# Decays laid out chunk by chunk, paired exponentials and 1 MB loads in a gated recurrence with a convolution-gated projection

## The chip, the cores and the metric

One core of a Trainium2 chip. The metric is the device time of one execution in microseconds (us); it is measured as the median of several runs. The program has five compute streams that run their own instruction queues in order and meet only at semaphores: TensorE (PE in the profile, with its weight loads as PEld), VectorE (DVE), ScalarE (ACT), GpSimd (POOL) and the queue that issues the DMAs (SP).

## The reference

Two layers over x of shape 4 x 6336 x 256 (batch, time, features), all float32.

```python
# layer 1: gated linear recurrence
a_base = 1/(1+exp(-a_param)); sig_r = 1/(1+exp(-r_gate)); sig_i = 1/(1+exp(-i_gate))
a_t  = exp(8 * sig_r * log(clip(a_base, 1e-6, 1-1e-6)))
norm = sqrt(max(1 - a_t*a_t, 1e-6))
h    = a_t[:, t] * h + (norm * sig_i * x)[:, t]        # over t; y[:, t] = h
# layer 2: on y
gate = 1/(1+exp(-causal_conv_5(y, conv_w)))            # 5 taps, each feature by itself
out  = (gate * (y @ w_val)) @ w_out
```

## The kernel before, in words

The 4 x 6336 = 25344 time steps stand in one row. They are cut into 51 windows (`w`, 512 steps, some 256) and 28 chunks (`c`): chunks 0, 1, 2, 26 and 27 are one window each, chunks 3 to 25 are two windows, 1024 steps. The 256 features are two halves `h` of 128.

Inputs arrive with time on the partitions. For a chunk the program does this, each step an operation with a short name in a hand-written order:

- `lr`, `li`, `lx` (SP): load a window of r_gate, i_gate and x, 512 KB, each partition a run of 4 rows (4 KB), into rings of four windows (`rring`, `iring`, `xring`).
- `ta`, `tb` (ACT): tanh of half the gates, for a whole chunk, to `taring` and `tbring` in bf16. The sigmoids are made from these.
- `tr` (PE): transposes of `taring`, so that features stand on the partitions; `ex` (ACT): the decays a_t = exp(k tanh + k), out of PSUM into `aring`, one instruction for each half of a chunk, or of a pair of chunks where `GROUPS` puts two together.
- `sq` (POOL): a squared, into `ering`; two of them are `sa`, on ACT. `rt` (ACT): sqrt(0.25 - 0.25 a²) for a batch of chunks (`BATCHES`, mostly three). Sqrt lies in another function table than tanh and exp, so an `ACT_TABLE_LOAD` stands before each batch and another before the next tanh or exp.
- `pp` (POOL): tanh + 1; `up` (POOL): times x, into `uring`. For three early windows PE and DVE do it (`xp`, `uv`).
- `nt` (PE): transposes of the square roots back to time on the partitions; two bf16 values are moved as one 4-byte element. `xg` (DVE): `uring` times them. `xt` (PE): transposes of that, features on the partitions. For the last two chunks (`LAST`) it is done the other way round.
- `sc` (DVE): the recurrence, a scan over a chunk for each half, into `yring`.
- `cv` (PE): the five taps as small diagonal matmuls; `tg` (ACT): tanh of it; `vl` (PE): y @ w_val; `gv` (DVE): (tanh + 1) times that; `ou` (PE): times w_out; `cd` (DVE) or `ca` (ACT): copy out of PSUM into `oring`; `st` (SP): store of a window, 512 KB.
- `wm` (PE): five matmuls of the identity, whose result nobody reads. There are 17 of them.

The table `ORDER` lists all operations in one sequence. Each engine executes its own in that sequence, so the table sets what stands behind what in each queue; semaphores put in by the framework do the rest. A word is `name.chunk.half` or `name.window`, and `@` gives the PSUM banks.

The transposes of `nt` read `ering` with a step, because time step and partition are dealt out by `p j`:

```python
nc.tensor.transpose(out=bank[:, k:k + P], in_=ering[:, e + q:e + wins[w] // 2:nq], identity=ident[:])
```

With windows of 512 steps nq is 2, so the 4-byte elements that are read lie 8 bytes apart; with 256 it is 1.

Of the kernel before, what the change touches and what calls it, by code (L numbers as in the profile page):

```python
# [9 lines left out]
P = 128  # L10
# [4 lines left out]
ALU = mybir.AluOpType  # L15

CHUNKS = [[256], [256], [512], [512, 512], [512, 512], [512, 512], [512, 512], [512, 512], [512, 512], [512, 512],
    [512, 512], [512, 512], [512, 512], [512, 512], [512, 512], [512, 512], [512, 512], [512, 512], [512, 512],
    [512, 512], [512, 512], [512, 512], [512, 512], [512, 512], [512, 512], [512, 512], [512], [256]]
BATCHES = [[0], [1], [2], [3, 4], [5, 6, 7], [8, 9, 10], [11, 12, 13], [14, 15, 16], [17, 18, 19], [20, 21, 22],  # L20
    [23, 24, 25], [26, 27]]
NA = 5120
# [16 lines left out]
s_ident s_small s_kt s_diag lr.2 lr.0 s_wl.3 lr.1 li.0 lr.3 s_wl.2 ta.2 ta.0 lr.4 tr.0.1@0 tr.2.0@1 lr.6 ta.1 lr.5  # L39
tr.1.0@2 tb.0 tr.0.0@3 li.1 tr.2.1@4 ex.2.0 li.2 tr.1.1@5 li.3 ex.1.1 lx.0 ex.0.1 sq.1.1 li.4 ex.1.0 sq.2.0 ex.0.0  # L40
ex.2.1 sq.1.0 ta.3 sq.2.1 pp.0 sq.0.0 sq.0.1 ta.4 tb.1 lr.10 tr.3.0@4,5 tb.2 lr.9 lr.8 lr.7 lx.2 tr.3.1@2,3 ex.3.0
s_wl.1 up.0 lx.1 lx.4 wm.10@6 ex.3.1 sq.3.0 wm.5@6 lx.3 wm.3@6 tb.3 sq.3.1 wm.9@6 wm.6@6 ta.6 pp.4 sq.4.1 ta.5 lr.13
li.5 xp.2@2,3 li.6 sq.4.0 li.7 lr.14 tr.5.0@4,5 lx.6 uv.2 pp.3 rt.0 rt.2 nt.0@0 up.4 xg.0 rt.1 xt.0@0,1 xp.1@2 rt.3
sc.0.0 nt.1@3 up.3 lx.5 nt.2@0 uv.1 s_wl.0 xg.1 xg.2 xt.1@2,3 sc.0.1 lx.7 sc.1.0 nt.3@6,7 lr.12 sc.1.1 xg.3 ex.5.0
xt.2@0,1 sc.2.1 sc.2.0 tb.4 cv.0@2,3 tr.5.1@4,5 xt.3@6,7 lr.11 li.8 sq.5.0 ex.5.1 tg.0 sc.3.0 pp.5 sc.3.1 cv.2@0,1
s_wcast cv.1@4,5 ta.8 xp.6@2,3 uv.6 vl.0@6,7 tg.1 tg.2 vl.2@0,1 up.5 ta.7 sq.6.1 lx.8 li.9 li.10 lr.17 lr.18
nt.4@2,3 gv.0 tb.5 tr.7.0@6,7 ou.0.0@4 gv.2 ex.7.0 xg.4 sq.6.0 cd.0.0 tr.7.1@0,1 sq.5.1 vl.1@2,3 ou.2.0@4,5 ex.7.1
# [59 lines left out]
def kernel(  # L107
# [34 lines left out]
    def places(cap, lens):  # L142
# [6 lines left out]
        return out  # L149

    group_of = {c: g for g in GROUPS for c in g}
    a_at = places(NA, clen)
    e_at = places(NE, clen)

    segs, y_at, y_wrap = [], [], []
# [34 lines left out]
    with tc.manual_schedule():  # L190
# [103 lines left out]
        def op_lr(w):  # L294
            load(w, "r")
# [298 lines left out]
```

## Time and profile before

| | |
|---|---|
| median of 3 runs | 287.65 us (287.34, 287.65, 289.22) |
| span of the profiled execution | 286.4 us; its own time is not listed apart, so the median of the runs, 1.25 us more, stands for it |
| busy: PE, DVE, ACT, POOL | 251.8, 246.8, 273.6, 241.6 us |
| bytes moved | 104.76 MB, mean 366 GB/s; HBM read 78.39 MB, written 25.95 MB |
| granted TensorE clock, mean | 0.999 |

The busy time of an engine is the union of its instructions, from the profiler; an instruction can start before the one ahead of it has ended, so the durations of a group add up to more. Idle time before an instruction is put down to what ended it. The chain of waits follows the work back from the last instruction. Times in the views count from the first instruction of the span.

### The profile page before, as it was taken

What the parts mean: (1) busy time and instruction counts of PE and PEld (TensorE: products, weight loads), DVE (VectorE), ACT (ScalarE), POOL (GpSimd) and SP (SyncE); (2) the same over time, 40 slices, a digit from 0 to 9 for tenths busy, and PEclk for the clock granted to TensorE, in tenths of its full rate; (3) what the DMA queues carried; (4) which work ended last, traced back from release to release, by engine and by line L of the source; (5) the groups of instructions that cost most, each with busy time, mean ns of one, the idle gap of its engine ahead of it and who ended that gap; (6) DMA issues with size and microseconds to landing.
All of it is one profiled execution on the core that took longest, in us unless ns stands there. A gap on an engine that the chain in (4) does not pass through costs nothing.

```text
span 286.4 us, 6382 instructions
## 1 busy us (share of the span) xinstructions
PE 251.8 (88%) x2552; PEld 171.1 (60%) x2576; DVE 246.8 (86%) x214; ACT 273.6 (96%) x198; POOL 241.6 (84%) x161
## 2 busy tenths in 40 slices
PE   1387778899999999988988999989989899999993
PEld 1253447456656767455756676656646774767562
DVE  4002898969999899999999999999999999999991
ACT  5999999999999999999999999999999999898984
POOL 1659589899999999999999999999996999874600
PEclk9999999999999999999999999999999999999999
DMA  7999999999999999999999999999999999994536
GB/s 243 384 373 407 409 403 408 388 366 376 410 408 366 418 367 392 414 410 334 405 364 413 411 332 356 420 416 419 415 401 333 359 416 406 364 356 170 192 150 256
DMA packets 29996, 104.76 MB, mean 366 GB/s; under 512 B 3335, under 2 KB 3854, under 8 KB 29966
## 3 DMA queue, kind: packets, MB, share of 16 engines
q1 hardware_dynamic: 29952, 104.35, 94.5%
q8 instruction: 20, 0.33, 0.5%
q14 instruction: 10, 0.08, 0.1%
q10 hardware_dynamic: 14, 0.01, 0.0%
HBM read 78.39 MB, written 25.95 MB: 364 GB/s over the span
## 4 chain that ended last, share of the span: by engine, by line
ACT 33%; PE 29%; DVE 14%; issue 12%; DMA 8%; SPq 1%; ACTq 0%; DVEq 0%
ACT ering L405 8%; PE banks L495 8%; DVE yring L483 7%; PE banks L525 7%; DMA rring<-in_r_gate_dram 6%; ACT tgring L502 6%; ACT taring L310 5%; ACT tbring L313 5%; ACT aring L378 5%; PE banks L510 5%; PE banks L461 3%; DVE tgring L515 3%; PE banks L420 3%; ACT L562 3%; DVE oring L533 2%
## 5 line engine op out<-in xcount | busy, mean ns | idle before, releaser
L386 POOL TENSOR_TENSOR ering<-aring 128x1024 f32<-128x1024 f32 (+2 forms) x54 | 91.5, 1714 | 16.7 <-ACT aring L378 16.4
L332 POOL TENSOR_TENSOR uring<-tbring,xring 128x1024 bf16<-128x1024 bf16 (+1 forms) x48 | 101.1, 2119 | 3.6 <-DMA xring<-in_x_dram 3.1
L483 DVE TENSOR_TENSOR_SCAN yring<-aring,yring,banks 128x1024 bf16<-128x1024 f32 (+5 forms) x50 | 101.7, 2064 | 2.1 <-PE banks L461 1.9
L495 PE MATMUL banks<-yring,diag 64*64 64x512 bf16 (+7 forms) x1080 | 62.1, 361 | 2.3 <-ACT aring L378 1.6
L515 DVE SCALAR_TENSOR_TENSOR tgring<-tgring,banks 128x1024 bf16<-128x1024 bf16 (+1 forms) x51 | 59.1, 1178 | 4.0 <-PE banks L510 3.4
L320 POOL TENSOR_SCALAR tbring<-tbring 128x1024 bf16<-128x1024 bf16 (+1 forms) x48 | 49.1, 1032 | 6.8 <-ACT tbring L313 6.7
L378 ACT ACTIVATE aring<-banks,khf 128x2048 f32<-128x2048 bf16 (+3 forms) x38 | 54.2, 1476 | 0.4 <-PE banks L357 0.3
L525 PE MATMUL banks<-wo,tgring 128*128 128x256 bf16 x396 | 51.0, 274 | 3.7 <-DVE tgring L515 3.2
L502 ACT ACTIVATE tgring<-banks 128x1024 bf16<-128x1024 f32 (+1 forms) x51 | 50.2, 1011 | 2.0 <-PE banks L495 1.9
L510 PE MATMUL banks<-yring,wv 128*128 128x512 bf16 (+4 forms) x192 | 48.1, 359 | 3.7 <-ACT tgring L502 1.9
L310 ACT ACTIVATE taring<-rring 128x2048 bf16<-128x2048 f32 (+2 forms) x28 | 47.9, 1718 | 1.4 <-DMA rring<-in_r_gate_dram 1.4
L525 PEld LDWEIGHTS <-tgring 128*128 128x128 bf16 x396 | 41.2, 114 | 13.1 <-DVE tgring L515 8.8
L313 ACT ACTIVATE tbring<-iring 128x2048 bf16<-128x2048 f32 (+2 forms) x28 | 48.2, 1726 | 0.0
L405 ACT ACTIVATE ering<-ering 128x4096 bf16<-128x4096 f32 (+5 forms) x16 | 44.8, 2840 | 0.1
L495 PEld LDWEIGHTS <-diag 64*64 64x64 bf16 x1080 | 29.0, 106 | 25.6 <-issue 9.9
L533 DVE COPY oring<-banks 128x1024 f32<-128x1024 f32 (+1 forms) x36 | 41.9, 1182 | 1.4 <-PE banks L525 0.7
L357 PE MATMUL banks<-ident_b,taring 128*128 128x128 bf16 x396 | 29.9, 230 | 9.4 <-ACT taring L310 6.7
L357 PEld LDWEIGHTS <-taring 128*128 128x128 bf16 x396 | 26.5, 103 | 14.2 <-ACT taring L310 7.4
L510 PEld LDWEIGHTS <-wv 128*128 128x128 bf16 x216 | 19.7, 98 | 24.5 <-issue 10.3
L450 DVE TENSOR_TENSOR uring<-banks,uring 128x2048 bf16<-128x2048 bf16 (+2 forms) x26 | 29.4, 1134 | 3.5 <-PE banks L420 3.2
L420 PE MATMUL banks<-ident,ering 128*128 128x128 f32 x192 | 28.3, 289 | 1.1 <-ACT ering L405 0.9
L461 PE MATMUL banks<-ident,uring 128*128 128x128 f32 x192 | 25.9, 276 | 3.5 <-DVE uring L450 2.8
(49 smaller groups left out, 154.0 us busy)
## 6 DMA issues: line engine op xcount, KB each, us to landing
rring<-in_r_gate_dram SPq DMA_DIRECT2D x48, 512.0 KB, 8.2
iring<-in_i_gate_dram SPq DMA_DIRECT2D x48, 512.0 KB, 8.7
xring<-in_x_dram SPq DMA_DIRECT2D x48, 512.0 KB, 8.2
out_dram<-oring SPq DMA_DIRECT2D x48, 512.0 KB, 6.5
rring<-in_r_gate_dram SPq DMA_DIRECT2D x3, 256.0 KB, 4.1
iring<-in_i_gate_dram SPq DMA_DIRECT2D x3, 256.0 KB, 6.5
xring<-in_x_dram SPq DMA_DIRECT2D x3, 256.0 KB, 8.5
out_dram<-oring SPq DMA_DIRECT2D x3, 256.0 KB, 5.2
```

Source lines behind the costliest of these rows:

```text
L310: nc.scalar.activation(**tangent(c, taring, NTR, rring, NRI))
L313: nc.scalar.activation(**tangent(c, tbring, NTI, iring, NII))
L332: nc.gpsimd.tensor_tensor(out=u, in0=t1, in1=xt, op=ALU.mult)
L378: nc.scalar.activation(out=dst, in_=src, func=ACT.Exp, scale=khf[:, h:h + 1], bias=khf[:, h:h + 1])
L386: nc.gpsimd.tensor_tensor(out=e, in0=a, in1=a, op=ALU.mult)
L405: nc.scalar.activation(out=ering[:].bitcast(BF16)[:, 4 * o:4 * o + 2 * n], in_=ering[:, 2 * o:2 * o + 2 * n], func=ACT.Sqrt, scale=-0.25, ...
L483: nc.vector.tensor_tensor_scan(out=yring[:, h, col:col + o1 - o0], data0=aring[:, h, a_at[c] + o0:a_at[c] + o1], data1=xT[:, o0:o1], initi ...
L495: nc.tensor.matmul(out=gp[oh * 64:oh * 64 + 64, h, a:b], lhsT=diag[half * 64:half * 64 + 64, h, k, :], rhs=yring[half * 64:half * 64 + 64, ...
L502: nc.scalar.activation(out=tgring[:, w % NTG, :, 0:wins[w]], in_=live.pop(("gp", w))[:, :, 0:wins[w]], func=ACT.Tanh, scale=0.5)
L510: nc.tensor.matmul(out=val[:, m, a:b], lhsT=wv[:, hk, m * P:(m + 1) * P], rhs=yring[:, hk, col:col + b - a], start=(hk == 0), stop=(hk == ...
L515: nc.vector.scalar_tensor_tensor(out=tgring[:, w % NTG, :, 0:wins[w]], in0=tgring[:, w % NTG, :, 0:wins[w]], scalar=1.0, in1=live.pop(("va ...
L525: nc.tensor.matmul(out=ops[:, j * D:(j + 1) * D], lhsT=gv[:, hk, j:wins[w]:J], rhs=wo[:, hk, :], start=(hk == 0), stop=(hk == H - 1))
```

## The change

- Loads: one DMA for a chunk of r_gate, i_gate or x in place of one for each window. A partition gets 8 consecutive rows, 8 KB, so a chunk of two windows is dealt out as one unit of 1024 steps (1 MB).
- Because of this, `tr`, `nt` and `xt` deal out a chunk as a unit too: in a chunk of 1024 steps the step nq of the reads of `nt` and of the writes of `xt` is 4, so that elements lie 16 bytes apart.
- `aring` holds both halves of a chunk side by side (`decays`), 6144 steps in place of 5120, at places given by a table `A_AT`. `oring` has 5 windows in place of 7.
- `GROUPS` has pairs throughout from chunk 3 to 24; chunks 11, 12, 21 and 22 were single.
- `sq` takes both halves of a chunk in one instruction, `pc` does the work of `pp` for a chunk. `sa` and `wm` are gone.
- `ORDER` is written anew.

Core of the diff:

```diff
-NA = 5120
+NA = 6144
-NOSB = 7
+NOSB = 5
-GROUPS = [[0], [1], [2], [3, 4], [5, 6], [7, 8], [9, 10], [11], [12], [13, 14], [15, 16], [17, 18], [19, 20], [21],
-    [22], [23, 24], [25], [26], [27]]
+GROUPS = [[0], [1], [2], [3, 4], [5, 6], [7, 8], [9, 10], [11, 12], [13, 14], [15, 16], [17, 18], [19, 20], [21, 22],
+    [23, 24], [25], [26], [27]]
+A_AT = [5120, 5376, 5632, 0, 1024, 2048, 3072, 4096, 5120, 0, 1024, 2048, 3072, 4096, 5120, 0, 1024, 2048, 3072, 4096,
+    5120, 0, 1024, 2048, 3072, 4096, 5120, 5632]
...
-        aring = rings.tile([P, H, NA], FP32, name="aring")
+        aring = rings.tile([P, H * NA], FP32, name="aring")
...
-        def load(w, which):
...
-            nc.sync.dma_start(dst, flat[which][wstart[w]:wstart[w] + n, :].rearrange("(p j) d -> p j d", p=P))
+        def load(c, which):
+            w, k, n = cwins[c][0], len(cwins[c]), clen[c]
+            ring, slots = {"r": (rring, NRI), "i": (iring, NII), "x": (xring, NX)}[which]
+            at = place(w, slots)
+            dst = ring[:, at:at + k, 0:wins[w] // P, :].rearrange("p w j d -> p (w j) d")
+            nc.sync.dma_start(dst, flat[which][cstart[c]:cstart[c] + n, :].rearrange("(p j) d -> p j d", p=P))
...
+        def op_pc(c):
+            w, k = cwins[c][0], len(cwins[c])
+            t = tbring[:, place(w, NTI):place(w, NTI) + k, 0:wins[w] // P, :].rearrange("p w j d -> p (w j d)")
+            nc.gpsimd.tensor_scalar(out=t, in0=t, scalar1=1.0, scalar2=1.0, op0=ALU.mult, op1=ALU.add)
...
-        def op_wm(k, at):
-            for _ in range(5):
-                nc.tensor.matmul(out=banks[:, at], lhsT=ident_b[:], rhs=ident_b[:].unsqueeze(1).to_broadcast([P, 4, P]),
-                                 start=True, stop=True)
...
+            dst = aring[:, H * at[0]:H * (at[0] + n * len(at))].rearrange("c (k h q j) -> c k h q j", h=H, j=J, k=len(at))
+            dst = dst[:, :, h]
             nc.scalar.activation(out=dst, in_=src, func=ACT.Exp, scale=khf[:, h:h + 1], bias=khf[:, h:h + 1])
...
-        def op_sq(c, h):
-            e, a = squares(c, h)
+        def both_squares(c):
+            n = clen[c]
+            return ering[:, H * e_at[c]:H * (e_at[c] + n)], aring[:, H * a_at[c]:H * (a_at[c] + n)]
+
+        def op_sq(c, *h):
+            e, a = squares(c, h[0]) if h else both_squares(c)
             nc.gpsimd.tensor_tensor(out=e, in0=a, in1=a, op=ALU.mult)
...
-                        nc.tensor.transpose(out=bank[:, k:k + P], in_=ering[:, e + q:e + wins[w] // 2:nq], identity=ident[:])
+            nq = n // (2 * P)
+            for q in range(nq):
+                for h in range(H):
+                    e = live["n", c] + h * n // 2
+                    nc.tensor.transpose(out=bank[:, k:k + P], in_=ering[:, e + q:e + n // 2:nq], identity=ident[:])
...
-st.50
+cv.50@4,5 ou.49.0@2,3 ca.48.0 st.48 tg.50 vl.50@0,1 ca.49.0 gv.50 ou.50.0@3 ca.50.0 st.49 st.50
```

Three places of the queues, before and now. First ACT's queue around `rt.10`, the square roots of chunks 23, 24 and 25 (the row of 128x6144). `taring` and `tbring` rows are `ta` and `tb`, `aring` rows `ex`, `tgring` rows `tg`, COPY rows `ca`, `ering<-aring` is `sa`. Before:

```order
L378 ACTIVATE aring<-banks,khf 128x2048
L378 ACTIVATE aring<-banks,khf 128x1024 x2
L394 ACTIVATE ering<-aring 128x1024
L313 ACTIVATE tbring<-iring 128x2048
L502 ACTIVATE tgring<-banks 128x1024
L313 ACTIVATE tbring<-iring 128x2048
L502 ACTIVATE tgring<-banks 128x1024 x2
L562 ACT_TABLE_LOAD
L405 ACTIVATE ering<-ering 128x6144
L562 ACT_TABLE_LOAD
```

And now:

```order
L299 ACTIVATE taring<-rring 128x512
L366 ACTIVATE aring<-banks,khf 128x1024
L366 ACTIVATE aring<-banks,khf 128x256
L366 ACTIVATE aring<-banks,khf 128x1024
L519 COPY oring<-banks 128x1024
L302 ACTIVATE tbring<-iring 128x2048
L486 ACTIVATE tgring<-banks 128x1024
L519 COPY oring<-banks 128x1024
L486 ACTIVATE tgring<-banks 128x1024 x2
L546 ACT_TABLE_LOAD
L393 ACTIVATE ering<-ering 128x6144
L546 ACT_TABLE_LOAD
```

The square on ACT is gone from this place; two copies, and the tanh and one exponential of the last chunk (128x512 and 128x256), have come ahead of the square roots.

Second, ACT's queue at the start, from the first square roots (`rt.0`, 128x512) on. Before, all of chunks 0 to 4 stand in one batch:

```order
L562 ACT_TABLE_LOAD
L405 ACTIVATE ering<-ering 128x512
L405 ACTIVATE ering<-ering 128x1024
L405 ACTIVATE ering<-ering 128x512
L405 ACTIVATE ering<-ering 128x4096
L562 ACT_TABLE_LOAD
```

Now chunks 3 and 4 (128x4096) have their own, after ten other instructions:

```order
L393 ACTIVATE ering<-ering 128x512
L546 ACT_TABLE_LOAD
L302 ACTIVATE tbring<-iring 128x1024
L366 ACTIVATE aring<-banks,khf 128x2x1024
...
L302 ACTIVATE tbring<-iring 128x2048
L546 ACT_TABLE_LOAD
L393 ACTIVATE ering<-ering 128x4096
L546 ACT_TABLE_LOAD
```

The table is changed once more there and back: two more loads of it than before. The first roots also stand nearer to the start of the queue.

Third, DVE's queue around `xg.23`, the product that waits for `rt.10` and `nt.23` (the first row `TENSOR_TENSOR uring` in each piece). Rows `tgring` are `gv`, rows `oring` are `cd`, rows `yring<-aring` are the scans. Before:

```order
L515 SCALAR_TENSOR_TENSOR tgring<-tgring,banks 128x1024
L533 COPY oring<-banks 128x1024 x2
L450 TENSOR_TENSOR uring<-banks,uring 128x2048
L515 SCALAR_TENSOR_TENSOR tgring<-tgring,banks 128x1024 x2
L450 TENSOR_TENSOR uring<-banks,uring 128x2048
L478 TENSOR_REDUCE yring<-yring 128x2x4
L483 SCALAR_TENSOR_TENSOR yring<-aring,yring,banks 128x1024 x2
```

And now:

```order
L499 SCALAR_TENSOR_TENSOR tgring<-tgring,banks 128x1024 x3
L517 COPY oring<-banks 128x1024 x3
L437 TENSOR_TENSOR uring<-banks,uring 128x2048
L499 SCALAR_TENSOR_TENSOR tgring<-tgring,banks 128x1024 x2
L437 TENSOR_TENSOR uring<-banks,uring 128x2048
L462 TENSOR_REDUCE yring<-yring 128x2x4
L467 SCALAR_TENSOR_TENSOR yring<-aring,yring,banks 128x1024 x2
```

From `xg.23` to the end of the queue the same instructions stand there as before (26 products, gates and scans, and two tiny reductions); ahead of it stand three gates and three copies in a row.

More of the change, by code (lines that the diff above doesn't have):

```diff
@@ L38 @@
 ORDER = """
[L39 to L43, printed above, removed]
@@ L151 @@
     group_of = {c: g for g in GROUPS for c in g}
-    a_at = places(NA, clen)
+    a_at = A_AT
     e_at = places(NE, clen)
```

237 lines of the change are left out of this document (105 added, 132 removed).

## Prediction

> **What bounds the kernel now.** I read the page's busy times first, then busy time by stretch, the chain of waits of the last stretch, and the groups of instructions by form.
>
> ```profile
> PE 251.8 (88%) x2552; PEld 171.1 (60%) x2576; DVE 246.8 (86%) x214; ACT 273.6 (96%) x198; POOL 241.6 (84%) x161
> HBM read 78.39 MB, written 25.95 MB: 364 GB/s over the span
> ```
>
> Everything is busy, ACT most at 96%. An average does not tell who leads, so the next view cuts the span at the points where ACT's queue changes character (columns: stretch, its length, busy us and instructions of PE, PEld, DVE, ACT, POOL, granted clock, DMA share, GB/s).
>
> ```profile
> 0.00:11.10 11.10, 2.66 (x19) 2.08 (x19) 3.80 (x20) 7.50 (x13) 2.79 (x10) 1.00 0.83 287
> 11.10:237.57 226.47, 205.42 (x2088) 140.00 (x2108) 201.34 (x160) 225.37 (x148) 214.33 (x135) 1.00 1.01 391
> 237.57:244.21 6.64, 6.46 (x69) 3.49 (x67) 6.53 (x7) 6.61 (x2) 6.64 (x6) 1.00 1.01 406
> 244.21:286.39 42.18, 37.30 (x377) 25.55 (x382) 35.10 (x29) 34.13 (x37) 17.84 (x13) 0.99 0.66 245
> ```
>
> From 11.1 to 237.6 us ACT is idle for 1.1 us in all, PE for 21, DVE for 25, POOL for 12: ACT's queue sets the pace, although the DMA share is 1.01 too. In the last 42.18 us ACT idles for 8. The chain of waits (start, length, what) says what happens there:
>
> ```profile
> 237.57 1.28 ACT L562
> 238.87 5.34 ACT ering L405
> 244.25 1.24 PE banks L420 x8
> 245.59 0.93 DVE uring L450
> ...
> 281.43 0.70 DVE tgring L515
> 282.17 0.63 PE banks L525 x4
> 282.82 0.58 ACT oring L535
> ```
>
> The table load at 237.57 and the 5.34 us behind it are rt.10, the square roots of chunks 23 to 25. When they end at 244.21, nt.23 (PE) and xg.23 (DVE) follow, and then the rest of the chain runs on PE and DVE to the last copy and its store. So the span is a sum of two queues: **ACT's queue up to the end of rt.10, 244.2 us, and 42.2 us from there**. In the second part DVE has the 26 instructions from xg.23 on, 36.5 us from 245.59 to 282.13 (281.43 and its 0.70), and waits between them for 2.7 us, mostly for PE.
>
> **The change part by part.** First what stands in ACT's queue up to the end of rt.10. Its prices (busy and mean ns of one stand behind the bar):
>
> ```profile
> L378 ACT ACTIVATE aring<-banks,khf 128x2048 f32<-128x2048 bf16 x18 | 36.8, 2074 | 0.0
> L378 ACT ACTIVATE aring<-banks,khf 128x1024 f32<-128x1024 bf16 x10 | 11.4, 1219 | 0.0
> L394 ACT ACTIVATE ering<-aring 128x1024 f32<-128x1024 f32 x1 | 1.1, 1122 | 0.0
> L313 ACT ACTIVATE tbring<-iring 128x2048 bf16<-128x2048 f32 x23 | 44.3, 1927 | 0.0
> L502 ACT ACTIVATE tgring<-banks 128x1024 bf16<-128x1024 f32 x48 | 48.6, 1037 | 2.0 <-PE banks L495 1.9
> L535 ACT COPY oring<-banks 128x1024 f32<-128x1024 f32 x14 | 13.9, 1016 | 2.1 <-PE banks L525 2.0
> L562 ACT ACT_TABLE_LOAD x18 | 23.1, 1283 | 0.3
> L310 ACT ACTIVATE taring<-rring 128x512 bf16<-128x512 f32 x3 | 1.9, 621 | 0.2 <-DMA rring<-in_r_gate_dram 0.2
> L378 ACT ACTIVATE aring<-banks,khf 128x256 f32<-128x256 bf16 x6 | 3.1, 570 | 0.3 <-PE banks L357 0.3
> ```
>
> - Four more pairs of exponentials for eight singles: 4 x 2.074 - 8 x 1.219 = -1.46 us.
> - The square sa.25.1 goes to POOL: -1.12.
> - Six copies stand ahead of rt.10 where three stood: 3 x 1.016 = +3.05.
> - Square roots in two batches at the start where one stood: two table loads, 2 x 1.283 = +2.57.
> - The tanh and one exponential of the last chunk have moved ahead of rt.10: 0.62 + 0.57 = +1.19.
>
> Together **+4.2 us**. ACT had 1.1 us of idle time in that stretch, so nothing hides this. Over the whole queue ACT gains 1.5 from the exponentials and 1.5 from both squares, and pays 2.6 for tables and 2.0 for copies (16 of that form for 14): 275.2 us of work for 273.6.
>
> At the start ACT's first tanh now needs a load of 256 KB, where it waited for 512 KB:
>
> ```profile
> 4.54 1.58 ACT L310 ACTIVATE taring<-rring 128x1024 bf16<-128x1024 f32 x2 [0.49 <-DMA rring<-in_r_gate_dram]
> 29.94 0.69 DVE L483 TENSOR_TENSOR_SCAN yring<-aring,banks 128x256 bf16<-128x256 f32 x1 [0.41 <-PE banks L461]
> ```
>
> At most the 0.49 us of that wait can be saved; I take **-0.4**. The first square roots come some 10 us earlier in the queue, so the first scan, now at 29.94, does too. That gives DVE a lead, but the last 26 instructions of DVE hang on rt.10, which is ACT's; the lead is spent in waiting. For the same reason I cost at nothing the two copies fewer on DVE (2.4 us) and POOL's savings:
>
> ```profile
> L386 POOL TENSOR_TENSOR ering<-aring 128x1024 f32<-128x1024 f32 x45 | 84.4, 1896 | 6.1 <-ACT aring L378 5.8
> L386 POOL TENSOR_TENSOR ering<-aring 128x512 f32<-128x512 f32 x4 | 4.2, 1039 | 2.9 <-ACT aring L378 2.9
> L320 POOL TENSOR_SCALAR tbring<-tbring 128x1024 bf16<-128x1024 bf16 x46 | 47.8, 1050 | 6.8 <-ACT tbring L313 6.7
> L320 POOL TENSOR_SCALAR tbring<-tbring 128x512 bf16<-128x512 bf16 x2 | 1.2, 619 | 0.0
> ```
>
> Doubling from 512 to 1024 adds 0.86 and 0.43 us, so a form twice as long again should take 1.90 + 2 x 0.86 = 3.61 for 3.79 and 1.91 for 2.10: about 0.18 saved for each of 45 instructions, 8 us, less the 2.5 us of the two squares that came from ACT. What covers it is ACT's queue; if POOL led, it would be a gain. The reverse matters too: sq.24, sq.23 and sq.25, 10.8 us, must end before rt.10 starts. From tb.23, which POOL's queue waits for just ahead of them, ACT has the next thirteen of its queue to do up to the table load, by the rows above 2.07 + 1.93 + 0.62 + 1.22 + 0.57 + 1.22 + 1.02 + 1.93 + 1.04 + 1.02 + 2 x 1.04 + 1.28 = 16.0 us, and POOL 1.91 + 10.8 = 12.7: 3 us to spare.
>
> Next the reads of nt, 16 bytes apart for 8. No row shows 16. The two nearest are the weight loads of nt (8 bytes) and of xt (side by side), as a group and eight in a row:
>
> ```profile
> L420 PEld LDWEIGHTS banks<-ident,ering 128*128 128x128 f32 x192 | 25.4, 207 | 5.8 <-issue 2.2 <-ACT ering L405 1.8 <-ACT oring L535 0.4
> L461 PEld LDWEIGHTS banks<-ident,uring 128*128 128x128 f32 x192 | 21.2, 141 | 8.8 <-DVE uring L450 6.7 <-DVE yring L472 0.8 <-issue 0.4
> 125.00 1.04 PEld L420 LDWEIGHTS banks<-ident,ering 128*128 128x128 f32 x8 [0.39 <-ACT ering L405]
> 127.62 0.86 PEld L461 LDWEIGHTS banks<-ident,uring 128*128 128x128 f32 x8 [1.02 <-DVE uring L450]
> ```
>
> From 4 to 8 bytes a load went from 141 to 207 ns, eight in a row from 0.86 to 1.04 us. Going to 16 bytes costs between nothing and twice that step of 66 ns, 132 ns each, 1.06 us for a chunk's eight. I take the middle, 0.55. The three chunks behind rt.10: nt.23 stands wholly on the path, nt.24 and nt.25 half (PE is busy 37.30 of 42.18 us): **+1.1**, ends 0 and 3.2. In the stretch before, 20 chunks x 0.55 = 11 us on PE, which is more than covered by the removed wm:
>
> ```profile
> 17.90 6.31 PE L364 MATMUL banks<-ident_b 128*128 128x512 bf16 x25
> L364 PE MATMUL banks<-ident_b 128*128 128x512 bf16 x85 | 21.1, 389 | 1.1 <-ACT aring L378 0.7 <-DVE yring L483 0.3
> 13.08 1.03 PE L357 MATMUL banks<-ident_b,taring 128*128 128x128 bf16 x8 [4.49 <-ACT taring L310]
> 27.69 1.06 PE L357 MATMUL banks<-ident_b,taring 128*128 128x128 bf16 x16
> ```
>
> The Trainium skill, "SBUF — State Buffer", section "Door 1: The DMA port swizzle", speaks against this part: it gives SBUF lines of 16 bytes, wants two hits in a line, and says that each access to a new line pays. At 8 bytes two elements share a line, at 16 none do, so by it the upper end holds: +3.2 in place of +1.1. The rows show a cost already at 8 bytes, which the rule calls free.
>
> xt writes PSUM with the same wider step. Its group above, already with 8 bytes between written elements, is the quicker of the two; a step such as nt's, 0.18 us a chunk, would be the upper end, and I take nothing. PE's queue behind nt.23 has one convolution in place of an output product, a value product and a transpose: 1.2 - 0.9 - 0.9 - 0.1, **-0.6**.
>
> Last the DMAs. 69 loads fewer save SP's issue time, and 8 KB pieces halve the packets. ACT waited for r_gate 1.4 us in the whole run (first row below), so I cost a better rate at nothing; ACT's queue hides it. Against that, `oring` has 5 windows for 7, and a store in SP's queue waits for the copy ahead of it:
>
> ```profile
> ACT taring L310 <- DMA rring<-in_r_gate_dram: 1.4, 4, 0.5
> SPq L546 <- DVE oring L533: 39.2, 19, 5.4
> out_dram<-oring SPq DMA_DIRECT2D x48, 512.0 KB, 6.5
> ```
>
> A window takes about 226.47/41 = 5.5 us, so 5 windows are 27 us; a wait of 5.4 us and a landing of 6.5 fit twice. Nothing. The loads queued behind such a store are for two chunks on, four windows or 22 us ahead.
>
> **Sum against the profiled execution:** 286.4 + 4.2 - 0.4 + 1.1 - 0.6 = 290.7 us of span. The median of the runs shown is 287.65, 1.25 above the span, so the prediction is **291.9 us**. Its own range: ACT's part between +3.5 and +4.3 (the copies and the moved tanh may fall into gaps), nt between 0 and 3.2, PE between -0.6 and 0: 289.5 to 294.5.
>
> **Rivals.**
>
> A, *the last stretch closes up*. nt costs nothing more and DVE's 2.7 us of waits behind rt.10 shrink to 0.5, because the three gates and three copies that now run during rt.10 leave PE less behind it. For: DVE has the same 26 instructions there, and some of PE's are gone. Against: the waits were for PE, busy 37.30 of 42.18. 286.4 + 4.2 - 0.4 - 0.6 - 2.2 = 287.4, time 288.6; range 286.5 to 290.5.
>
> B, *the DMA engines led all along* (the other side, faster). For: share 1.01 in the long stretch, so no DMA engine is ever idle, and an ACT whose inputs just arrive looks busy. Against: ACT's wait for r_gate is 1.4 us. If 8 KB pieces brought the loads, three quarters of the bytes (78.39 of 104.34 MB), from the 391 GB/s of the long stretch to the 406 of the next, 226.47 x 0.75 x (1 - 391/406) = 6.3 us go from the span: 280.1, time 281.4. It decides where ACT's rows ahead of rt.10 get shorter, which my sum excludes.
>
> By the Trainium skill, "DMA: Bandwidth & Descriptors", section "Rules for kernel authors", loads should be at least 1 MiB each, which is what this rival would reward; with 406 GB/s in 512 KB loads the trace leaves little for it.
>
> C, *ACT runs dry in the middle*. Each gate tanh waits for its convolution, that for the scan, that for nt. If nt costs 1.06 more a chunk and a third of it is not covered, 20 chunks lose 7 us: time 298.9, range 294.5 to 306. For: every engine runs above 88% there, so a new order has little play. Against: PE is relieved of 21.1 us of wm.
>
> D, *PE's clock falls where wm is missing*. The rows at 13.08 and 27.69 show transposes 0.13 us apart before the 25 wm at 17.90, and 0.066 after. If PE ran so slowly for a quarter of the last stretch, its 37.3 us of work would grow by 9: 300.9 us. Against: there was no wm in that stretch before either, at a granted clock of 0.99. The Trainium skill's "TensorE: Matmul & The Clock Gate", section "Why this matters for your kernels", warns of idle gaps above some 3 us; the stretches of the early windows could have them, where DVE's lead hides the cost.
>
> **How the numbers follow.** Forecast 0.45, A 0.27, B 0.10, C 0.14, D 0.04. About 1%, 2.9 us, is what a measurement tells from no change: the bounds are 284.8 and 290.5. Faster is B, 0.10. A and a fifth of the forecast (between 289.5 and 290.5) are the same, 0.36. The rest of the forecast, C and D are slower, 0.54. A range from 286.0 to 300.0 leaves out B and the far part of C and D, about 0.18.
>
> **What would show it.** rt.10 should end at about 248, with ACT idle under 2 us from 11 us to there; xg.23 to the end should take 42 to 43 us with the same 26 DVE instructions. nt's weight loads should read between 207 and 340 ns, POOL's long squares near 3.6 us, PE's clock 1.00. The forecast is wrong if rt.10 ends before 245 (B), if ACT shows more than 4 us of idle time ahead of it (C), or if the last stretch is below 40.5 us (A).

## Result and the profile after

| | before | after |
|---|---|---|
| median of the runs, us | 287.68 (287.34 to 289.22) | 296.86 (296.18 to 299.82) |
| ratio | | 1.0327 [1.0266, 1.0389] |
| span of the profiled execution, us | 286.4 | 294.4 |

The change is slower by 9.2 us. The forecast was 291.9: the direction was right, and more than half of the size was missed. Executions of the changed kernel scatter over some 3 us and more, those of the kernel before over 1 to 2; ratios leave out executions over 1.5% above the fastest of their kernel.

The page's parts on transfers and clock (kernel after; the clock row has one digit for each fortieth of the span, in tenths of full speed):

```profile
PEclk9999999799997999999999999999999999999998
DMA packets 20057, 104.73 MB, mean 356 GB/s; under 512 B 2231, under 2 KB 2750, under 8 KB 11198
q1 hardware_dynamic: 20016, 104.34, 90.7%
```

A third of the packets is gone, as the diff says. New are the two 7s in the clock row, at 52 to 59 and 88 to 96 us, and the 8 at the end; before it had 9 throughout.

The same cut by stretches as in the prediction, at 11.1 us and around the square roots of batch 10 (kernel after; columns as there):

```profile
0.00:11.10 11.10, 2.77 (x19) 1.92 (x19) 3.80 (x20) 7.23 (x12) 3.74 (x11) 1.00 0.83 301
11.10:245.13 234.03, 193.39 (x2006) 133.27 (x2027) 200.99 (x158) 229.93 (x151) 209.10 (x92) 0.99 0.96 379
245.13:251.76 6.63, 6.42 (x59) 4.15 (x57) 6.63 (x7) 6.61 (x2) 6.63 (x4) 1.00 1.01 353
251.76:294.40 42.64, 36.71 (x382) 25.10 (x388) 34.89 (x29) 32.17 (x33) 17.73 (x13) 0.98 0.63 241
```

ACT's column is the fourth busy time. Up to the end of rt.10 ACT works 7.23 + 229.93 + 6.61 = 243.77 us, before 7.50 + 225.37 + 6.61 = 239.48: **+4.3**. Its idle time in the first 11.1 us went from 3.60 to 3.87, **+0.3**, and in the long stretch from 1.10 to 4.10, **+3.0**. The last stretch went from 42.18 to 42.64, **+0.5**. Together 8.0 us of span. The other 1.2 lie in the choice of executions: where both are listed, a run's time stands some 1.9 us above its own span, so the medians belong to spans near 285.8 and 295.0; the profiled execution of before was a long one, that of after a short one.

The groups of instructions by form (after; busy, mean ns of one), in the order in which the prediction priced them:

```profile
L366 ACT ACTIVATE aring<-banks,khf 128x2048 f32<-128x2048 bf16 x22 | 44.8, 2068 | 0.0
L519 ACT COPY oring<-banks 128x1024 f32<-128x1024 f32 x16 | 16.2, 1021 | 1.6 <-PE banks L509 1.4
L546 ACT ACT_TABLE_LOAD x20 | 25.7, 1283 | 0.4
L382 POOL TENSOR_TENSOR ering<-aring 128x2048 f32<-128x2048 f32 x23 | 82.5, 3601 | 4.5 <-ACT aring L366 4.1 <-PE banks L406 0.4
L315 POOL TENSOR_SCALAR tbring<-tbring 128x2048 bf16<-128x2048 bf16 x22 | 41.7, 1899 | 13.8 <-ACT tbring L302 13.8
L406 PEld LDWEIGHTS banks<-ident,ering 128*128 128x128 f32 x192 | 25.2, 208 | 9.5 <-issue 3.5 <-ACT ering L393 2.8 <-DVE uring L437 0.8
```

Prices came out as worked out (squares 3.60 for 3.61, additions 1.90 for 1.91), but for the last row: nt's weight loads, now in 16-byte steps, take 208 ns for 207. By the Trainium skill's "SBUF — State Buffer", section "Door 1: The DMA port swizzle", every one of these elements lies in a line of its own and should have cost more; the trace does not agree.

ACT's waits for loads and for other engines up to the end of rt.10, the first 3 us left out (rows of ACT's timeline; the bracket holds the idle time and its releaser), after and then before from 11.1 us on:

```profile
3.41 0.63 ACT L299 ACTIVATE taring<-rring 128x512 bf16<-128x512 f32 x1 [0.39 <-DMA rring<-in_r_gate_dram]
4.95 1.58 ACT L299 ACTIVATE taring<-rring 128x1024 bf16<-128x1024 f32 x2 [0.91 <-DMA rring<-in_r_gate_dram]
10.56 1.91 ACT L299 ACTIVATE taring<-rring 128x2048 bf16<-128x2048 f32 x1 [1.04 <-DMA rring<-in_r_gate_dram]
13.56 1.91 ACT L299 ACTIVATE taring<-rring 128x2048 bf16<-128x2048 f32 x1 [0.42 <-DMA rring<-in_r_gate_dram]
54.57 1.02 ACT L486 ACTIVATE tgring<-banks 128x1024 bf16<-128x1024 f32 x1 [0.29 <-PE banks L479]
56.71 1.02 ACT L486 ACTIVATE tgring<-banks 128x1024 bf16<-128x1024 f32 x1 [1.11 <-PE banks L479]
87.64 1.91 ACT L299 ACTIVATE taring<-rring 128x2048 bf16<-128x2048 f32 x1 [1.61 <-DMA rring<-in_r_gate_dram]
235.98 2.76 ACT L366 ACTIVATE aring<-banks,khf 128x1024 f32<-128x1024 bf16 x3 [0.20 <-DVE oring L517]
```

```profile
13.40 1.91 ACT L310 ACTIVATE taring<-rring 128x2048 bf16<-128x2048 f32 x1 [0.38 <-DMA rring<-in_r_gate_dram]
24.55 1.91 ACT L310 ACTIVATE taring<-rring 128x2048 bf16<-128x2048 f32 x1 [0.28 <-DMA rring<-in_r_gate_dram]
```

From 11.1 us on, gate tanh waits 1.40 us for convolutions where it did not wait, r_gate 2.03 us for 0.66, and an exponential 0.20: together the 3.0 us. The waits at 54 to 57 and at 87.6 us are what the experiments look into. Times below are medians, ratios are to the kernel before on the same chip, whose median was 287.49 to 287.80 us in all rounds.

### The profile page after: what moved, and what is told of

The parts are those of the page before. It is cut to its first block, busy times and chain, and to the rows that moved or that the text cites. A ratio compares the mean times of both kernels' runs of the same rounds, so it can differ in the third digit from the quotient of the medians.

```text
span 294.4 us, 6030 instructions
## 1 busy us (share of the span) xinstructions
PE 239.3 (81%) x2464; PEld 164.4 (56%) x2491; DVE 246.3 (84%) x212; ACT 275.9 (94%) x196; POOL 237.2 (81%) x118
## 4 chain that ended last, share of the span: by engine, by line
ACT 37%; DVE 17%; PE 15%; DMA 13%; issue 13%; POOL 2%; SPq 1%; ACTq 0%; DVEq 0%
DMA rring<-in_r_gate_dram 10%; DVE yring L467 8%; ACT ering L393 7%; ACT tgring L486 7%; ACT tbring L302 6%; ACT aring L366 6%; ACT taring L299 5%; PE banks L494 5%; ACT L546 5%; PE banks L479 4%; DVE tgring L499 3%; DVE oring L517 3%; PE banks L509 3%; DMA iring<-in_i_gate_dram 3%; DVE uring L437 2%
## 5 line engine op out<-in xcount | busy, mean ns | idle before, releaser
L382 POOL TENSOR_TENSOR ering<-aring 128x2048 f32<-128x2048 f32 (+2 forms) x33 | 90.0, 2747 | 11.1 <-ACT aring L366 10.7
L499 DVE SCALAR_TENSOR_TENSOR tgring<-tgring,banks 128x1024 bf16<-128x1024 bf16 (+1 forms) x51 | 59.3, 1182 | 14.7 <-PE banks L494 12.7
L479 PE MATMUL banks<-yring,diag 64*64 64x512 bf16 (+7 forms) x1080 | 63.5, 369 | 6.2 <-DVE yring L467 3.6
L494 PE MATMUL banks<-yring,wv 128*128 128x512 bf16 (+7 forms) x189 | 48.8, 369 | 13.1 <-ACT tgring L486 5.7
L366 ACT ACTIVATE aring<-banks,khf 128x2048 f32<-128x2048 bf16 (+3 forms) x34 | 52.9, 1598 | 0.2 <-DVE oring L517 0.2
L315 POOL TENSOR_SCALAR tbring<-tbring 128x2048 bf16<-128x2048 bf16 x22 | 41.7, 1899 | 13.8 <-ACT tbring L302 13.8
L479 PEld LDWEIGHTS <-diag 64*64 64x64 bf16 x1080 | 30.9, 108 | 29.8 <-issue 15.0
L517 DVE COPY oring<-banks 128x1024 f32<-128x1024 f32 (+1 forms) x34 | 39.7, 1185 | 2.7 <-PE banks L509 2.5
L352 PE MATMUL banks<-ident_b,taring 128*128 128x128 bf16 x396 | 28.7, 227 | 13.5 <-ACT taring L299 12.7
L352 PEld LDWEIGHTS <-taring 128*128 128x128 bf16 x396 | 24.8, 101 | 19.9 <-ACT taring L299 14.5
L406 PEld LDWEIGHTS banks<-ident,ering 128*128 128x128 f32 x192 | 25.2, 208 | 9.5 <-issue 3.5
```

Source lines behind the costliest of these rows:

```text
L366: nc.scalar.activation(out=dst, in_=src, func=ACT.Exp, scale=khf[:, h:h + 1], bias=khf[:, h:h + 1])
L382: nc.gpsimd.tensor_tensor(out=e, in0=a, in1=a, op=ALU.mult)
L479: nc.tensor.matmul(out=gp[oh * 64:oh * 64 + 64, h, a:b], lhsT=diag[half * 64:half * 64 + 64, h, k, :], rhs=yring[half * 64:half * 64 + 64, ...
L494: nc.tensor.matmul(out=val[:, m, a:b], lhsT=wv[:, hk, m * P:(m + 1) * P], rhs=yring[:, hk, col:col + b - a], start=(hk == 0), stop=(hk == ...
L499: nc.vector.scalar_tensor_tensor(out=tgring[:, w % NTG, :, 0:wins[w]], in0=tgring[:, w % NTG, :, 0:wins[w]], scalar=1.0, in1=live.pop(("va ...
```

## Experiments

### Copies back to VectorE (`e1_copies_on_dve`)

```diff
-ca.16.0 ca.18.0 ca.24.0 ca.29.0 ca.34.0 ca.35.0
+cd.16.0 cd.18.0 cd.24.0 cd.29.0 cd.34.0 cd.35.0
```

> The changed kernel with the six copies that stand on ACT ahead of rt.10 (windows 16, 18, 24, 29, 34, 35) given to DVE. Theory 1, ACT's queue up to rt.10 sets the time one for one: 6 x 1.02 = 6.1 us less on ACT, so rt.10 ends at about 246 for 251.8 and the time is about 290.8 for 296.9. Theory 2, from 100 us on DVE is the bound behind ACT (it idles 5.6 us there) and takes 7.3 us more: rt.10 ends above 249, the time is 294 or more.

303.63 us, 1.0542 [1.0509, 1.0575]. ACT is relieved and the kernel is slower by 6 to 7 us. ACT's waits for convolutions (over the whole execution: us, times, longest; 5.0, 6, 1.9 in the changed kernel):

```profile
ACT tgring L486 <- PE banks L479: 16.1, 14, 2.7
```

The gates wait 11 us more in sum. By the order, the copies now stand ahead of scans in DVE's queue, and the convolutions need the scans. ACT's work is not all that sets the pace.

### Filling matmuls at three holes, and one load earlier (`e2_three_wm`, `e3_load_earlier`)

```diff
+wm.0@0 behind nt.3, wm.1@0 behind xt.4, wm.2@0 behind tr.7.1      (e2)
-... li.9 ... st.6 lr.12 lr.13                                     (e3)
+... lr.12 li.9 ... st.6 lr.13
```

> The changed kernel with three of the removed wm put back where PE waits between 43 and 52 us (behind nt.3, xt.4 and tr.7.1). If the clock that fell to a mean of 0.83 in 50 to 60 us made the convolutions late for which ACT waited 1.40 us, the clock there is 1.00 again, those waits are gone, and the time is 1.4 to 3 us shorter (295.5 to 294). If PE was only waiting for the scans, the waits stay and the time is the same within 1 us.

> The changed kernel with the load of r_gate for chunk 12 ahead of the load of i_gate for chunk 9 and the store of window 6 in SP's queue. If its place behind those two made ACT wait 1.61 us at 87.6, that wait is gone and the time is 1 to 3 us shorter (296 to 294). If the load waits for its ring slots or for the DMA engines anyway, ACT waits as before and the time is the same within 1 us.

e2: 301.34 us (295.8 to 302.46), no gain; three of the four executions took 301 us or more. In the profiled one, the shortest, ACT's waits for convolutions at 54 to 57 us went from 1.40 to 0.89 and the r_gate wait near 87 from 1.61 to 0.59, but a wait of 0.94 for a convolution at 31.3 and one of 1.26 for r_gate at 142.9 are new: span 294.0. e3: 297.16, 1.0307 [1.0251, 1.0362], no gain: the r_gate wait at 87.6 us is gone, and an i_gate tanh waits 1.62 us at 86.0 for the load that stood behind.

### The order before on the new layout, with five staging windows (`e4_old_order`, `e5_layout_alone`)

```diff
-GROUPS and ORDER of the changed kernel
+GROUPS, ORDER, filling matmuls and per-half squares of the kernel before
+(e4) each load of 1 MB at the place of the second of the two it replaces
+(e5) each load of one window, 512 KB, at its old place
```

> The new layout and loads alone: chunks dealt out as a unit, 1 MB loads with 8 KB pieces, five staging windows, decays chunk by chunk and six deep, but the groups, the 17 wm, the squares by half, the additions by window and the order of the kernel before (each load at the place of its second window). Theory 1, the order and ACT's queue cost the time: 286 to 289 us, as the kernel before. Rival, the layout or the larger loads cost it: 293 or more.

> The order of instructions, the groups of exponentials and the filling matmuls of the kernel before, window for window, on the decay layout of the changed kernel (halves beside each other, 6 chunks, 5 staging windows, norm transposes in 16-byte steps). Each load is one window of 512 KB in 4 KB pieces, as before. If the layout, the 16-byte steps and the two staging windows fewer cost nothing outside the last stretch, as the prediction's sum has it: 287.5 to 288.8 us. If they carry the 3.3 us of ScalarE idle time that the prediction missed: 290.5 or more.

In both, stores 12, 24, 27, 29 and 30 leave behind the copy that takes their staging window next, so these five windows' outputs are a later window's; in e4 the x loads of chunks 10 and 23 also come behind the first use, so that it uses an earlier chunk's x. 320.17 us, 1.1147 [1.1104, 1.1191], and 303.57, 1.0551 [1.0523, 1.0578]. They mix the layout with five staging windows, for which that order was not made, and settle nothing; the next runs part the two.

### The layout with seven staging windows, and its halves (`e9_layout_seven`, `e11_seven_halves_apart`, `e10_layout_seven_whole`)

```diff
-NA = 6144, NOSB = 5                      (e9, on e5)
+NA = 5120, NOSB = 7, a_at = places(NA, clen)
-at = H * a_at[c] + h * clen[c]           (e11, on e9)
+at = h * NA + a_at[c]
-two loads of 512 KB for a chunk          (e10, on e9)
+one load of 1 MB, ahead of the first use
```

> The kernel before (its order, groups, filling matmuls, five chunks of decays and seven staging windows) on the new layout: a chunk's two halves side by side, eight input rows per partition of a chunk, norm transposes in 16-byte steps. Loads by window, 512 KB in 4 KB pieces. By the prediction's sum the layout costs at most the 16-byte steps behind batch 10: 287.5 to 288.8 us. If the layout itself slows an engine all along: 290 us or more.

> The run e9_layout_seven (295.5 us) with one thing put back: the two halves of the decays lie apart again, each half of all chunks in one stretch, as in the kernel before. The eight rows per partition, the 16-byte norm transposes and the order stay. Theory O, with the halves side by side the strided write of a pair of exponentials spans the other half's decays, so an exponential waits for a scan of the other half and a square for the other half's exponential: 287.5 to 288.5 us, no wait of an exponential for DVE, POOL's wait for exponentials back from 25.7 to about 16 us. Theory R, the new rows or the 16-byte steps cost it: 294 to 296 us.

> The run before it with each chunk's two loads joined into one of 1 MB in 8 KB pieces, at the place of the later of the two where the ring and the first reader allow it. ScalarE leads and the loads are hidden: 287.5 to 288.8 us. The DMA engines lead and larger pieces bring them on: 284 us or less. The later place of the first half makes ScalarE wait for it: 291 us or more.

e9: 295.52 us, 1.0264 [1.0242, 1.0286]. **On the old order the layout alone costs 7.7 us.** e11: 288.28, 1.0027 [1.0007, 1.0047]. With the halves apart nearly all of that is gone, so the eight rows for each partition and the 16-byte steps cost some 0.7 us. ACT and then DVE in e9:

```profile
135.91 2.06 ACT L380 ACTIVATE aring<-banks,khf 128x2048 f32<-128x2048 bf16 x1 [1.24 <-DVE yring L485]
```

```profile
133.47 2.34 DVE L485 TENSOR_TENSOR_SCAN yring<-aring,yring,banks 128x1024 bf16<-128x1024 f32 x1
```

By the order the exponential is ex.15.1 and the scan is sc.11.0: half 1 of chunks 15 and 16, written over the places of chunks 10 and 11, waits for a scan of half *0*, which reads no element that the exponential writes. But side by side, the strided write of a pair spans from half 1 of one chunk over half 0 of the next to its half 1. In the kernel before the same exponential ran while that scan was on (ACT, then DVE):

```profile
133.56 2.07 ACT L378 ACTIVATE aring<-banks,khf 128x2048 f32<-128x2048 bf16 x1
```

```profile
132.40 2.33 DVE L483 TENSOR_TENSOR_SCAN yring<-aring,yring,banks 128x1024 bf16<-128x1024 f32 x1
```

That the exponential waits because of this span is read from the places, and e11 bears it out. POOL's squares wait in the same way for the other half's exponential, and the square roots then for the squares (e9, waits of POOL and of ACT; e11, waits of POOL):

```profile
POOL ering L396 <- ACT aring L380: 25.7, 10, 7.6
ACT ering L411 <- POOL ering L396: 0.8, 1, 0.8
```

```profile
POOL ering L397 <- ACT aring L380: 15.6, 7, 7.3
```

In e9 rt.10 ends at 250.0 us for 244.2 and the rest takes 43.9 for 42.2.

e10: 298.6, 1.0357 [1.0325, 1.039], 3 us more than e9. The joined loads stand at the later place, and it is POOL's x that comes late: in the profiled execution POOL waits 12.7 us for x, in e9 4.1, and tanh of i_gate then waits for POOL, which it did not in e9:

```profile
ACT tbring L307 <- POOL uring L331: 4.1, 3, 2.9
```

Size and place of the loads changed together here, so this says nothing of the size alone.

### Halves apart in the new order (`e12_after_halves_apart`)

```diff
-at = H * a_at[c] + h * clen[c]
+at = h * NA + a_at[c]              (squares: two instructions for a chunk)
```

> The changed kernel with the halves of the decays apart, six chunks deep, and each chunk's squares therefore as two instructions at the same place (some 0.2 us more on GpSimd for each chunk). If the overlap of the halves also costs the changed kernel, in its new order, the 3.3 us of idle time that the prediction missed: 293 us. If the new order was made so that the overlap does not matter, and the order itself makes the idle time: 296 to 298 us.

297.95 us (293.64 to 299.65), 1.027 [1.0204, 1.0337]: the interval overlaps the changed kernel's, so no gain can be told. ACT's exponentials do not wait for scans in either: with six chunks the scans that read an exponential's place stand far ahead of it in the order. The profiled execution, the shortest of the four, shows what the new order can do: rt.10 ends at 249.5 us, ACT idles for 1.3 us from 11.1 us to there, and the span was 291.5 us at a granted clock of 0.999, where the changed kernel had 251.8, 4.1, 294.4 and 0.985. The forecast was 248, under 2 and 290.7. The other three executions had spans of 294.9 to 297.8. TensorE in e12, and then in the changed kernel, at the same place of the program (convolutions of windows 4, 3 and 6, behind the same hole of 1.92 us):

```profile
53.59 3.66 PE L480 MATMUL banks<-yring,diag 64*64 64x512 bf16 x58 [1.92 <-DVE yring L468]
```

```profile
52.85 5.12 PE L479 MATMUL banks<-yring,diag 64*64 64x512 bf16 x58 [1.92 <-DVE yring L467]
90.52 4.44 PE L494 MATMUL banks<-yring,wv 128*128 128x512 bf16 x11 [2.39 <-ACT tgring L486]
```

58 matmuls take 63 ns each in the one and 88 in the other, 1.46 us more, with ACT's gates behind them. The two last rows lie in the stretches of the two 7s (changed kernel, columns as above):

```profile
50.00:60.00 10.00, 7.83 (x78) 4.06 (x76) 4.93 (x3) 8.58 (x7) 8.07 (x4) 0.83 0.92 369
90.00:100.00 10.00, 9.23 (x71) 5.39 (x71) 7.30 (x6) 9.94 (x7) 8.43 (x5) 0.83 1.02 388
```

In the second ACT is busy for 9.94 of 10 us: that fall of the clock stands behind the r_gate wait and cost ACT nothing there.

### Filling matmuls in nine holes (`e15_after_nine_wm`), three cures at once (`e14_after_three_cures`), none in the kernel before (`e8_before_no_filling`)

```diff
+wm.0@0 cv.1, wm.1@2 xt.3, wm.2@2 tr.7.0, wm.3@4 cv.4, wm.4@6 ou.4.0,      (e15: each ahead
+wm.5@0 vl.6, wm.6@2 tr.9.0, wm.7@2 vl.8, wm.8@0 vl.12                       of the word named)
+e2's three wm and e3's lr.12, and li.10 ahead of st.6                      (e14)
-all 17 wm.k                                                               (e8, on before)
```

> The changed kernel with nine groups of five filling matmuls, one ahead of each instruction at which TensorE idled for 0.8 to 2.4 us between 28 and 110 us (convolution 1, xt.3, tr.7.0, convolution 4, output 4, values 6, tr.9.0, values 8, values 12). Theory D, the granted clock falls behind those holes and the convolutions then come late for ScalarE: no 10-us window under 0.95 in that part, and 293.5 us, as the one execution of the run with halves apart had it (span 291.5 at a clock of 0.999). Theory 2, the clock follows the waits and does not make them: 296 us or more.

> The changed kernel with the three groups of filling matmuls of the second run, the r_gate load of chunk 12 ahead of the i_gate load of chunk 9, and the i_gate load of chunk 10 ahead of the store of window 6: one cure for each of the waits of ScalarE at 54.6, 56.7 and 87.6 us and for the one that took its place. Theory 1, these waits are separate losses that add up: 3 us less idle time, 293.5 us. Theory 2, a wait that is cured comes back elsewhere since the queues of the new order are tight against each other: 296 us or more.

> The kernel before without its 17 groups of five filling matmuls. If they only fill holes, as the prediction took it with 0.96: 287.5 us. If they keep TensorE's clock up so that the convolution is in time for ScalarE: 290 us or more, with granted clock under 0.98 in 10-us windows of 30 to 100 us, as the changed kernel shows it there.

e15, by stretches of 10 us:

```profile
50.00:60.00 10.00, 8.49 (x102) 4.76 (x101) 5.99 (x4) 9.97 (x8) 9.60 (x4) 1.00 0.99 388
90.00:100.00 10.00, 9.20 (x86) 6.20 (x89) 9.01 (x8) 9.96 (x6) 7.44 (x4) 1.00 1.02 394
```

The clock (third number from the end) is 1.00 where it was 0.83, ACT is idle for under 0.05 us in each of these two stretches, its waits at 56.7 and 87.6 us are gone, and the profiled span is 292.9 for 294.4. But the median is 296.93, 1.0312 [1.0278, 1.0345], and executions with a granted clock of 1.000 had spans of 295.1 and 296.6. So the clock explains some 1.5 us of one execution, the waits for the slow convolutions, and not the time of the others. Why the r_gate wait at 87.6 us went too is not shown; the load itself was not moved. e14: 298.78, 1.0306 [1.0241, 1.0372], no gain either. Without wm the kernel before takes 288.01, 1.0011 [0.9988, 1.0035]: no worth of theirs can be told there.

### Loads of half the size (`e6_half_loads`)

```diff
-nc.sync.dma_start(ring[both windows], 1 MB)
+for v in the chunk's windows: nc.sync.dma_start(ring[window v], 512 KB)
```

> The changed kernel with each 1 MB load issued as two of 512 KB (4 KB pieces), both at the place of the one; the order stays. Theory 1, the size of the loads makes the transfers late and ScalarE idle: the 3.3 us of idle time go, 293.5 us. Theory 2, the order of the issues in SyncE's queue and the chain scan, convolution, tanh do it whatever the size: 296 to 298 us, as the changed kernel.

302.19 us, 1.046 [1.0392, 1.0527], slower than the changed kernel's 1.0327. ACT's waits for loads (r_gate, i_gate), over the whole execution, are 7.5 and 3.1 us for 4.4 and 1.1; the execution is the longest of the four (304.36 us), so they belong to more than the difference of the ratios:

```profile
ACT taring L298 <- DMA rring<-in_r_gate_dram: 7.5, 7, 1.7
ACT tbring L301 <- DMA iring<-in_i_gate_dram: 3.1, 2, 2.0
```

Both theories fell: large loads do not make the idle time, they spare this order some 4 us (by the ratios; the intervals just part).

### No stores (`e7_after_no_stores`, `e8_before_no_stores`)

```diff
-st.0 ... st.49
```

> The changed kernel without the stores of windows 0 to 49 (their output is left out); the copies into the staging windows stay. A quarter of the DMA bytes and every wait of SyncE's queue for a copy are gone. Theory 1, the transfers and SyncE's queue cause the 3.3 us of ScalarE idle time that the prediction missed: ScalarE idles some 4.7 us up to the end of the square roots of batch 10 (8.0 in the changed kernel), 292 to 293.5 us. Theory 2, the chain scan, convolution, gate tanh in the new order causes it: idle time stays at 7 us or more, 296 to 297 us.

> The kernel before without the stores of windows 0 to 49 (their output is left out). If ScalarE alone sets the pace there: 286.5 to 288 us, since ScalarE's work is the same. If the DMA engines, whose share is 1.01, set it together with ScalarE: 284 us or less.

Before without stores: 287.62, 0.9996 [0.9984, 1.0008]. A quarter of the bytes is worth nothing there, so the DMA share of 1.01 was no bound. After without them: 295.24 (294.49 to 295.82), 1.0253 [1.0231, 1.0275]: some 1.6 us less by the medians, at the edge of what the intervals tell apart, and a narrower scatter. In the profiled execution ACT idles for 7.8 us up to the end of rt.10, where the changed kernel has 8.0; the waits at 56.7 and 87.6 us are small or gone, and others stand in their place:

```profile
11.30 1.91 ACT L297 ACTIVATE taring<-rring 128x2048 bf16<-128x2048 f32 x1 [1.83 <-DMA rring<-in_r_gate_dram]
27.43 2.06 ACT L364 ACTIVATE aring<-banks,khf 128x2048 f32<-128x2048 bf16 x1 [1.15 <-PE banks L350]
57.31 2.11 ACT L484 ACTIVATE tgring<-banks 128x1024 bf16<-128x1024 f32 x2 [0.33 <-PE banks L477]
```

The idle time stays, so theory 1 of this run fell: the stores cost the new order some 1.6 us by the medians, which the intervals do not part from nothing, and the rest is not theirs.

### Five staging windows in the kernel before (`e13_before_five_windows`)

```diff
-NOSB = 7
+NOSB = 5      (st.12, 24, 27, 29, 30 right ahead of the next copy into their window)
```

> The kernel before with five staging windows for seven, and the five stores (12, 24, 27, 29, 30) that stood behind the next copy into their window moved ahead of it. By the prediction a store's wait fits twice: 287.5 to 288.3 us. If a store at an earlier place holds the loads behind it in SyncE's queue: 290 us or more.

299.79 us, 1.0397 [1.0346, 1.0448]. DVE's waits say how:

```profile
DVE oring L532 <- DMA out_dram<-oring: 7.8, 2, 5.0
```

Two copies wait for the whole landing of the store just ahead of them, up to 5.0 us, and TensorE and ACT's gates behind them (5.36 us at 211.12). Part of this is how the five stores were placed. In the profiled execution of the changed kernel no copy waits for a store; in that of e12 one does, for 1.6 us.

### Three copies more and three fewer on ScalarE (`e7_before_three_copies`, `e16_before_fewer_copies`)

```diff
-cd.16.0 cd.24.0 cd.29.0      (e7, on before)
+ca.16.0 ca.24.0 ca.29.0
-ca.19.0 ca.23.0 ca.33.0      (e16, on before)
+cd.19.0 cd.23.0 cd.33.0
```

> The kernel before with the copies of windows 16, 24 and 29 moved from VectorE to ScalarE (three more of about 1.02 us on ScalarE ahead of the sqrt of batch 10, three fewer on VectorE). Theory 1, ScalarE's queue sets the pace one for one, the largest term of the prediction: 290.5 us. Theory 2, ScalarE has slack there since it waits for VectorE and TensorE as often as they for it: 287.0 to 288.5 us.

> The kernel before with ScalarE's three copies ahead of the square roots of batch 10 (windows 19, 23 and 33) moved to VectorE. If ScalarE sets the pace alone: 3.0 us less, 284.6 us, which would beat both kernels. If VectorE, which has 25 us of idle time there, is as tight because the copies delay scans and gates behind them in its queue: 288 to 291 us.

e7: 292.47, 1.0158 [1.0132, 1.0185]: +4.7 us for 3.05 us of work. e16: 292.78, 1.0186 [1.0154, 1.0217]: **+5 us for 3.05 us less**. ACT's waits in e7 and in e16:

```profile
ACT oring L534 <- PE banks L524: 4.2, 6, 1.1
```

```profile
ACT aring L377 <- PE banks L356: 5.0, 4, 2.1
ACT aring L377 <- DVE yring L482: 1.3, 1, 1.3
```

Copies moved to ACT bring their own wait for the output product (4.2 us for 2.8 in the kernel before; the new waits stand at 135.0 and 198.0 us). 3.05 us of work and 1.4 of such waits are 4.4 of the 4.7. With copies moved away from ACT, exponentials, which had waited 0.3 us for TensorE, wait 5.0; that the copies delay DVE, and DVE the rest, is read from the order. The reading that fits both: in the kernel before ACT is busy all along because the others are just in time for it, and a move in either direction breaks that. No run fitted the rest of the order to the moved copies.

## Why the prediction was right in direction and wrong in size

- **ACT's work ahead of rt.10, +4.2.** Measured +4.3 in the profiled executions, and the prices of the rows held. As a price of time it is not shown: the same kind of copy, put on ACT in the kernel before, cost 4.7 us for 3.05 of work (e7), and taking six copies off ACT in the changed kernel made it slower (e1). "Nothing hides this" held; that each added instruction can also wait was left out.
- **ACT idle under 2 us from 11 us on.** This is the step that failed. The sum has no term for new waits in ACT's queue; it took 1.1 us of idle time to stay, and the profiled execution had 4.10. By the prediction's own mark (more than 4) that is rival C, but not by C's cause: nt costs no more (208 ns for 207). In its place stand late convolutions at 54 to 57 us (1.40 us), which go with the lower clock behind TensorE's holes, D in a small form (some 1.5 us by e12 and e15), and a late load at 87.6 us (1.61). One execution of e12 had none of them and idled for 1.3 us, so the sum priced the new order at its best, as far as one execution of a slightly different kernel tells.
- **The start, -0.4.** It came out as +0.3: the first tanh starts at 3.41 us for 4.54, but ACT's waits for r_gate in the first 11.1 us went from 0.72 to 2.34. Neither number can be told from scatter: the profiled executions had 3.2 to 4.2 us of idle time there with the old order, and 2.7 to 4.5 with the new one.
- **Last stretch, +1.1 - 0.6 = +0.5.** The sum held at +0.46, by luck. Its first term did not hold, as nt's loads cost nothing there, and the four prices behind the second add up to -0.7. The chain of waits of the changed kernel runs through a late load of i_gate instead:

```profile
255.43 9.05 DMA iring<-in_i_gate_dram
264.57 1.06 ACT L302 ACTIVATE tbring<-iring 128x1024 bf16<-128x1024 f32 x1 [1.13 <-DMA iring<-in_i_gate_dram]
```

  From the end of rt.10 to that of the last copy it is 39.6 us, before 39.2; in e12 and e15, where this wait is 0.5 us or none, 38.9. By these executions the relief of PE was worth some 0.3 us, and the late load cost some 0.6.
- **The layout at nothing on DVE and POOL.** The step asked only what the steps in bytes cost. It missed that two halves side by side put the strided write of one over the other: 7.7 us on the old order (e9), 0.7 with the halves apart (e11). The new order does not show it (e12).
- **DMAs and staging at nothing.** For the order before, taking out the stores changed nothing (287.62). In the new order the transfers are not wholly hidden: the late loads above, and some 4 us that larger loads save (e6); the stores cost 1.6 us or so, not told from nothing. "Fits twice" left out that a copy is held by the store's landing when the store stands close ahead of it (e13).
- **B, the DMA engines led.** Out: a quarter of the bytes less changed nothing. The Trainium skill's "DMA: Bandwidth & Descriptors", section "Rules for kernel authors", wants at least 1 MiB for each load. The time of e6 against the changed kernel agrees (302.19 us for 296.86), and e10 against e9 cannot tell, since the place of the loads changed with their size.
- **From span to median.** 1.25 us was taken; the profiled execution of before was some 0.6 long, so it should have been 1.9.
- **The range.** Its terms add up to 290.2 to 294.8 us, not 289.5 to 294.5. The measured 296.86 lies above either.

So the missing 5.0 us are 3.0 of ACT's idle time in the long stretch, 0.7 at a start that gained nothing, 1.2 from profiled executions that were long before and short after, and 0.1 of ACT's work. The idle time of the profiled execution is accounted for wait by wait, but no run that cured a wait shortened the median: the clock's part is some 1.5 us of that execution and none of the median, the stores' part some 1.6 us of the median and 0.2 of the idle time of the profiled one, and the copies' own waits (e7) are shown in the order before and not in the new one. Why the clock's cure does not shorten the median, and which waits fill the longer executions, stays open. No version here beats the kernel before.

## What to carry to other kernels

Where an engine is busy to 99% because the others are just in time for it, added work can cost more than its own instruction times (4.7 us for 3.05 here), and removed work can cost as much: price an added instruction with the wait that it can bring, and a removed one with what it puts in another queue. Give the sum a term for new waits when the whole order is rewritten. When two tiles are laid side by side, ask which strided writes now span the neighbour and what reads it, before asking about bytes. A cure of one wait in a tight order says nothing until the median has moved: here three cures (e2, e3, e15) shortened or removed the waits they aimed at, and none the median.

## What was not expected of the hardware

- A weight load in 16-byte steps took 208 ns, in 8-byte steps 207, side by side 141.
- TensorE's granted clock went to 0.83 in two 10-us windows with holes of 1.9 and 2.4 us (88 ns a matmul for 63 behind the first), and in an execution of e12 stayed at 1.00 in the 10 us around the same hole of 1.92. The Trainium skill's "TensorE: Matmul & The Clock Gate", section "Why this matters for your kernels", puts the danger at idle gaps above some 3 us; in this execution shorter ones were enough.
- In the kernel before, whose DMA engines show a share of 1.01 for 230 us, a quarter of the bytes could go without any change of time that could be measured (0.9996 [0.9984, 1.0008]).
